# Projecting Q for pairs of batches with 288 moving columns, with output pieces at alternating rates and half-unit score banks

## The chip, the cores and the metric

The kernel runs on one core of one Trainium2 chip. The metric is device time in microseconds (us) of that core. Executions fall into a fast and a slower state.

Names used below. TensorE is the matmul engine (PE in the profile, PEld for its weight loads), DVE the vector engine, ACT the scalar engine, POOL the GpSimd engine, SyncE (SP, SPq) the engine that issues all DMAs. A *unit* is one head of one batch of one problem: 2 problems x 16 batches x 16 heads = 512 units. A *K window* is the DMA that transposes K of 16 units, a *V slot* holds V of two units. An *output piece* is one 448-column matmul of the last projection. A matmul streams *moving columns* past weights loaded before. *pp* and *ps* are the two steps in which POOL adds up the probabilities of a unit before the sum matmul reads them. The *slack* of a load is the time from its landing to its first use. "The switch" is the stretch, units 224 to 287, in which the second problem's weights replace the first's.

## The reference

```python
# twice, for A and for B, with their own inputs; B=16, Sq=144, D=448, H=16, Sk=512, Dh=256, bf16
q = (x @ wq).reshape(B, Sq, H, Dh).transpose(0, 2, 1, 3)
scores = einsum("bhqd,bhkd->bhqk", q, k_cache) * (Dh ** -0.5)
p = softmax(scores, axis=-1)
o = einsum("bhqk,bhkd->bhqd", p, v_cache)
out = o.transpose(0, 2, 1, 3).reshape(B, Sq, H * Dh) @ wo
# result: concatenate([out_A, out_B], axis=-1)
```

## The kernel before

The program is recorded once into a list per engine by a small scheduler, which also derives every semaphore wait; each engine then plays its list in order. Per unit TensorE does eight matmuls of 144 columns for Q, eight for the scores, eight for P times V, one that sums the probabilities, and on average 2.25 output pieces. The parts that the change touches (cuts marked with `# ...`):

```python
LQ, LS = 6, 2                       # Q runs 6 units ahead of PV, the scores 2
NV, NXG = 9, 2                      # 9 V slots; 2 x slots of XB batches
XB = 4 if Bn % 4 == 0 else (2 if Bn % 2 == 0 else 1)
NQT, NPT, NPP, NPS, NRI, NOST, NRUN = 6, 3, 2, 3, 2, 2, 32
# ... PSUM: qp_ps 1 bank, s_ps 2 x 2 banks, ot_ps 2, op_ps 1: all 8 banks

def t_q(U):                          # Q of one unit: 8 matmuls of 144 columns
    for kc in range(4):
        for dc in range(2):
            t.matmul(qp_ps[:, dc * SQ:(dc + 1) * SQ], lhsT=wq_sb[:, kc, c0:c0 + 128],
                     rhs=xt_sb[:, xsl, kc, xo:xo + SQ], start=(kc == 0 and dc == 0), stop=(kc == 3), ...)
def t_evac_q(U):                     # DVE: 288 elements per partition, PSUM to SBUF
    v.tensor_copy(qt_sb[:, U % NQT, :, :], src)

def t_exp(U):                        # ACT: one exp of 576 elements over two score banks
    a.activation(pt_sb[:, psl, ...], s_ps[bank][:, :, 0:2 * SQ], AF.Exp, scale=DH ** -0.5)

def t_presum(U):                     # POOL: adds the four key chunks of P, in two steps
    g.tensor_tensor(pp_sb[:, pl, :, :], pt_sb[:, psl, 0:2, :], pt_sb[:, psl, 2:4, :], op=ALU.add)
    g.tensor_tensor(ps_sb[:, sl, :], pp_sb[:, pl, 0, :], pp_sb[:, pl, 1, :], op=ALU.add)

# the loop that fixes the order, i = unit of PV
while True:
    # ... DMA issues that are due at i, stores
    t_q(i + LQ); t_evac_q(i + LQ)
    t_s(i + LS); t_exp(i + LS); t_presum(i + LS)
    t_pv(i); t_sum(i)                # the sum matmul reads ps_sb
    t_recip(i); t_check(i); t_evac_ot(i)   # ACT Ln, Exp; DVE check, ring multiply
    credit += OP_RATE                # 1.15 x the mean number of output pieces per unit
    # ... emit output pieces, two at a time, while credit and ready pieces last;
    # ... each fourth piece of the first problem's last chunk issues one of the second's eight wo loads
```

At the end every engine reads a flag and branches over a fallback path; SyncE waits for the last stores before it branches.

## Time and profile before

| | before |
|---|---|
| time, median of 3 runs | 1091.85 us (1091.58 to 1093.75) |
| span of the profiled execution | 1095.4 us |
| TensorE busy | 95% |

The head of the page of the kernel before: the span, the busy time of each engine with its share and number of instructions, and the chain of waits by engine.

```profile
span 1095.4 us, 33206 instructions
...
PE 1036.4 (95%) x13952; PEld 924.4 (84%) x13952; DVE 657.9 (60%) x2215; ACT 620.3 (57%) x1573; POOL 623.3 (57%) x1029
...
PE 88%; SPq 7%; DMA 3%; DVE 1%; ACT 1%; issue 0%; DVEq 0%
```

TensorE is the limit: it is on 88% of the chain that ended last, and every other engine is under 61% busy. But busy time does not say how tightly matmuls follow one another. The timeline of TensorE does (start and duration in us, then engine, line, operation, tiles and count):

```profile
499.82 0.35 PE L1111 MATMUL op_ps<-wo_sb,ring 128*128 128x448 bf16 x1
500.01 0.66 PE L940 MATMUL qp_ps<-xt_sb,wq_sb 128*128 128x144 bf16 x8
500.51 0.66 PE L965 MATMUL s_ps<-qt_sb,kt_sb 128*128 128x144 bf16 x8
501.01 0.66 PE L1012 MATMUL ot_ps<-pt_sb,v_sb 128*128 128x144 bf16 x8
```

Read the starts, not the durations (which overlap). Eight 144-column matmuls take 0.50 us from start to start, 62.5 ns each; the output piece took 499.82 to 500.01, 0.19 us. Both are columns / 2.4 GHz + 2.5 ns. This gives a ruler: take each matmul's start, subtract it from the next one's start, and subtract columns / 2.4 GHz + 2.5 ns. What is left is time that TensorE lost there, to a wait or to a lowered clock. I call it *lost time* below. In the kernel before, from 120 to 540 us, the lost time is 0.1 us in all. It lies elsewhere:

| us | sum of columns/2.4 + 2.5 ns | before first matmul | start (units 0 to 63) | switch (units 224 to 287) | all other units | from the last matmul's start to the end | span |
|---|---|---|---|---|---|---|---|
| before | 1017.7 | 11.0 | 41.0 | 16.8 | 0.5 | 8.3 | 1095.4 |

What the losses at the switch are made of is in the list of waits (engine, tile and line, who ended the wait: total us, times, longest):

```profile
PE s_ps L965 <- DMA kt_sb<-in_B_k_cache_dram: 6.7, 1, 6.7
...
PE qp_ps L940 <- DMA wq_sb<-in_B_wq_dram: 2.3, 1, 2.3
PE ot_ps L1012 <- DMA v_sb<-in_B_v_cache_dram: 2.1, 2, 1.9
```

Most of the rest of the 16.8 us, 3.9 us, is half clock: after these idle stretches 64 matmuls run at half the pace, those of 144 columns starting 120 ns apart instead of 62.5. Finally the groups of instructions that the change edits (line, engine, operation, tiles, shape, count; busy us, mean ns of one; idle before them and what ended it):

```profile
L987 POOL TENSOR_TENSOR pp_sb<-pt_sb 128x288 f32<-128x288 bf16 x512 | 373.1, 729 | 419.1 <-ACT pt_sb L977 418.9
L977 ACT ACTIVATE pt_sb<-s_ps 128x576 bf16<-128x576 f32 x512 | 332.9, 650 | 433.0 <-PE s_ps L965 433.0
...
L991 POOL TENSOR_TENSOR ps_sb<-pp_sb 128x144 bf16<-128x144 f32 x512 | 249.9, 488 | 40.1
L952 DVE CAST qt_sb<-qp_ps 128x288 bf16<-128x288 f32 x512 | 225.0, 440 | 44.1 <-PE qp_ps L940 41.3
```

Off TensorE everything has room: POOL needs 729 + 488 ns in a unit of about 2 us, the cast 440 ns.

### The profile page before, as it was taken

Reading aid. Unit: us, or ns where it says so; the run is one execution under the profiler, and the core shown is the slowest. Engines: PE = TensorE matmul, PEld = TensorE weight load, DVE = VectorE, ACT = ScalarE, POOL = GpSimd, SP = SyncE. Lnnn points to the kernel's source line nnn. Section 1 sums busy time; section 2 is a strip of 40 time slices with the busy share of each in tenths; the row PEclk is TensorE's granted clock in tenths of the full one; section 3 lists DMA queues with packets and bytes.
Section 4 is the critical chain, followed back from the end, with each engine's and each line's share of the span. In section 5 each row is a group of like instructions: output and inputs, shape, how many; then the busy total and the mean of one; then the engine's idle time right before and its main releaser. Section 6 shows DMA issues by size and latency. Waiting matters only on the chain.

```text
span 1095.4 us, 33206 instructions
## 1 busy us (share of the span) xinstructions
PE 1036.4 (95%) x13952; PEld 924.4 (84%) x13952; DVE 657.9 (60%) x2215; ACT 620.3 (57%) x1573; POOL 623.3 (57%) x1029
## 2 busy tenths in 40 slices
PE   1859999999999999999999799999999999999997
PEld 1858888888988889999988688889998888999995
DVE  1526666666666666666656446666666666666663
ACT  0526565565655665666656445566665556666663
POOL 0526555556655566666646446566665655666663
PEclk9969999999999999999999989999999999999999
DMA  9999999999999999999999999999999999999930
GB/s 231 297 322 275 256 279 283 281 275 284 267 265 289 280 282 276 293 282 266 259 301 311 279 288 290 286 285 286 294 287 254 278 260 269 270 288 264 261 137 13
DMA packets 631519, 294.20 MB, mean 269 GB/s; under 512 B 549440, under 2 KB 562240, under 8 KB 631360
## 3 DMA queue, kind: packets, MB, share of 16 engines
q1 hardware_dynamic: 631360, 291.99, 110.1%
q8 instruction: 111, 1.82, 0.7%
q14 instruction: 48, 0.39, 0.1%
HBM read 148.90 MB, written 4.13 MB: 140 GB/s over the span
## 4 chain that ended last, share of the span: by engine, by line
PE 88%; SPq 7%; DMA 3%; DVE 1%; ACT 1%; issue 0%; DVEq 0%
PE ot_ps L1012 22%; PE qp_ps L940 22%; PE s_ps L965 22%; PE op_ps L1111 19%; SPq L915 5%; PE ot_ps L1024 3%; DMA v_sb<-in_A_v_cache_dram 1%; DMA wq_sb<-in_B_wq_dram 1%; DMA v_sb<-in_B_v_cache_dram 1%; SPq L925 1%; SPq L894 1%; PE qp_ps L1111 1%; DVE run_sb L1069 0%; ACT pt_sb L977 0%; DVE qt_sb L952 0%
## 5 line engine op out<-in xcount | busy, mean ns | idle before, releaser
L987 POOL TENSOR_TENSOR pp_sb<-pt_sb 128x288 f32<-128x288 bf16 x512 | 373.1, 729 | 419.1 <-ACT pt_sb L977 418.9
L977 ACT ACTIVATE pt_sb<-s_ps 128x576 bf16<-128x576 f32 x512 | 332.9, 650 | 433.0 <-PE s_ps L965 433.0
L1069 DVE TENSOR_REDUCE run_sb<-ot_ps 1x1 bf16<-1x144 f32 x1024 | 262.2, 293 | 384.2 <-ACT ln_sb L1035 384.2
L940 PEld LDWEIGHTS qp_ps<-xt_sb,wq_sb 128*128 128x128 bf16 x4096 | 293.0, 99 | 113.9 <-issue 27.5
L940 PE MATMUL qp_ps<-xt_sb,wq_sb 128*128 128x144 bf16 x4096 | 345.7, 228 | 29.3 <-DMA wq_sb<-in_A_wq_dram 24.0
L965 PE MATMUL s_ps<-qt_sb,kt_sb 128*128 128x144 bf16 x4096 | 343.9, 228 | 12.6 <-DMA kt_sb<-in_B_k_cache_dram 6.7
L1012 PE MATMUL ot_ps<-pt_sb,v_sb 128*128 128x144 bf16 x4096 | 343.1, 227 | 9.2 <-DMA v_sb<-in_A_v_cache_dram 7.1
L965 PEld LDWEIGHTS s_ps<-qt_sb,kt_sb 128*128 128x128 bf16 x4096 | 277.9, 99 | 13.7 <-DMA kt_sb<-in_B_k_cache_dram 6.9
L1012 PEld LDWEIGHTS ot_ps<-pt_sb,v_sb 128*128 128x128 bf16 x4096 | 276.8, 99 | 10.7 <-DMA v_sb<-in_A_v_cache_dram 7.7
L1111 PE MATMUL op_ps<-wo_sb,ring 128*128 128x448 bf16 x1120 | 285.1, 353 | 0.0
L991 POOL TENSOR_TENSOR ps_sb<-pp_sb 128x144 bf16<-128x144 f32 x512 | 249.9, 488 | 40.1
L952 DVE CAST qt_sb<-qp_ps 128x288 bf16<-128x288 f32 x512 | 225.0, 440 | 44.1 <-PE qp_ps L940 41.3
L1055 DVE TENSOR_TENSOR ring<-ot_ps,rinv_sb 128x288 bf16<-128x288 f32 (+2 forms) x640 | 231.0, 375 | 0.0
L1040 ACT ACTIVATE rinv_sb<-ln_sb 128x144 f32<-128x144 f32 x512 | 165.4, 323 | 16.2
L1035 ACT ACTIVATE ln_sb<-ot_ps 128x144 f32<-128x144 f32 x512 | 148.6, 290 | 14.8 <-PE ot_ps L1024 14.8
L1024 PE MATMUL ot_ps<-ps_sb,ones 128*128 128x144 bf16 x512 | 116.3, 227 | 0.0
L1111 PEld LDWEIGHTS op_ps<-wo_sb,ring 128*128 128x128 bf16 x1120 | 94.0, 98 | 21.4 <-DVE ring L1055 0.4
L1024 PEld LDWEIGHTS ot_ps<-ps_sb,ones 128*128 128x128 bf16 x512 | 50.4, 98 | 0.0
L1129 ACT ACTIVATE ost_sb<-op_ps 128x448 bf16<-128x448 f32 x35 | 18.5, 529 | 2.4 <-PE op_ps L1111 2.3
L1111 PE MATMUL qp_ps<-wo_sb,ring 128*128 128x448 bf16 x32 | 7.2, 352 | 0.0
L1111 PEld LDWEIGHTS qp_ps<-wo_sb,ring 128*128 128x128 bf16 x32 | 3.1, 98 | 2.9
L1075 DVE TENSOR_REDUCE runs_sb<-run_sb 1x1 f32<-1x32 bf16 x32 | 4.5, 169 | 0.0
(13 smaller groups left out, 5.1 us busy)
## 6 DMA issues: line engine op xcount, KB each, us to landing
v_sb<-in_A_v_cache_dram SPq DMA_DIRECT2D x128, 512.0 KB, 8.0
v_sb<-in_B_v_cache_dram SPq DMA_DIRECT2D x128, 512.0 KB, 6.8
out_dram<-ost_sb SPq DMA_DIRECT2D x36, 112.0 KB, 6.3
wo_sb<-in_A_wo_dram SPq DMA_DIRECT2D x8, 448.0 KB, 7.1
wo_sb<-in_B_wo_dram SPq DMA_DIRECT2D x8, 448.0 KB, 8.4
wq_sb<-in_A_wq_dram SPq DMA_DIRECT2D x4, 768.0 KB, 6.8
wq_sb<-in_B_wq_dram SPq DMA_DIRECT2D x4, 768.0 KB, 9.0
wq_sb<-in_A_wq_dram SPq DMA_DIRECT2D x4, 128.0 KB, 7.6
```

The costliest lines, as they stand in the source:

```text
L940: ins = t.matmul(qp_ps[:, dc * SQ:(dc + 1) * SQ], lhsT=wq_sb[:, kc, c0:c0 + 128], rhs=xt_sb[:, xsl, kc, xo:xo + SQ], start=(kc == 0 and dc ...
L952: return v.tensor_copy(qt_sb[:, sl, :, :], src)
L965: ins = t.matmul(s_ps[bank][:, c // 2, (c % 2) * SQ:(c % 2 + 1) * SQ], lhsT=kt_sb[:, 2 * c + dc, ko:ko + 128], rhs=qt_sb[:, U % NQT, dc, : ...
L977: return a.activation(pt_sb[:, psl, :, :].rearrange("p (a b) q -> p a (b q)", a=2), s_ps[bank][:, :, 0:2 * SQ], AF.Exp, scale=DH ** -0.5)
L987: return g.tensor_tensor(pp_sb[:, pl, :, :], pt_sb[:, psl, 0:2, :], pt_sb[:, psl, 2:4, :], op=ALU.add)
L991: return g.tensor_tensor(ps_sb[:, sl, :], pp_sb[:, pl, 0, :], pp_sb[:, pl, 1, :], op=ALU.add)
L1012: ins = t.matmul(ot_ps[ob][:, dc * SQ:(dc + 1) * SQ], lhsT=v_sb[:, vsl, j, c * DH + dc * 128:c * DH + (dc + 1) * 128], rhs=pt_sb[:, sl, c, ...
L1024: return t.matmul(ot_ps[ob][:, 2 * SQ:3 * SQ], lhsT=ones[:, :], rhs=ps_sb[:, sl, :], start=True, stop=True)
L1040: return a.activation(rinv_sb[:, sl, :], ln, AF.Exp, scale=-1.0)
L1055: ins = v.tensor_tensor(ring[:, 2 * h:2 * h + 2, r0:r0 + q1 - q0], ot_ps[ob][:, 0:2 * SQ].rearrange("p (c q) -> p c q", c=2)[:, :, q0:q1], ...
L1069: return v.tensor_reduce(run_sb[0:1, k, j:j + 1], ot_ps[ob][0:1, 2 * SQ:3 * SQ], axis=AX.X, op=op)
L1111: ins = t.matmul(acc[0:m, 0:D], lhsT=ring[:, c, col0:col0 + m], rhs=wo_sb[:, c, :], start=(c == first), stop=(c == last))
```

## The change

The intent: the same wq block serves two batches, so project Q for an even batch and the odd one after it together, with 288 moving columns per weight load: half the Q matmuls and half their weight loads. Even batches then carry all of Q, odd ones none, and the output pieces are given rates of 0.3 (even) and 2.0 (odd) to level the load. Q for 16 waiting heads needs 19 q slots and a second Q bank in PSUM. To pay for them, the score banks shrink to three of half a unit (with two exps of 288 elements per unit), x keeps one slot for two, pp one for two, ps two for three, and Ln shares its buffer with the reciprocal. With two ps buffers, the presum of a unit must be recorded after the sum matmul two units back, whose buffer it takes, so it moves behind the sum in the loop. Apart from that, SyncE's wait for the last stores moves behind the branch.

```diff
-    LQ, LS = 6, 2
+    LQ, LS = 4, 2
-    NV, NXG = 9, 2
+    NV, NXG = 9, 1
-    NQT, NPT, NPP, NPS, NRI, NOST, NRUN = 6, 3, 2, 3, 2, 2, 32
+    NQ0, NPT, NPS, NRI, NOST, NRUN = 3, 3, 2, 2, 2, 32
 ...
-        qt_sb = sb("qt_sb", [128, NQT, 2, SQ], BF16)
+        qt_sb = sb("qt_sb", [128, NQ0 + H, 2, SQ], BF16)
-        pp_sb = sb("pp_sb", [128, NPP, 2, SQ], F32)
+        pp_sb = sb("pp_sb", [128, 2, SQ], F32)
-        qp_ps = ps("qp_ps", [128, 512], F32)
-        s_ps = [ps("s_ps%d" % i, [128, 2, 512], F32) for i in range(2)]
+        qp_ps = ps("qp_ps", [128, 2, 512], F32)
+        s_ps = [ps("s_ps%d" % i, [128, 512], F32) for i in range(3)]
 ...
-                for kc in range(4):
-                    for dc in range(2):
+                for dc in range(2):
+                    for kc in range(4):
                         c0 = h * DH + dc * 128
-                        ins = t.matmul(qp_ps[:, dc * SQ:(dc + 1) * SQ], lhsT=wq_sb[:, kc, c0:c0 + 128],
-                                       rhs=xt_sb[:, xsl, kc, xo:xo + SQ], start=(kc == 0 and dc == 0),
-                                       stop=(kc == 3), skip_group_check=True)
+                        ins = t.matmul(qp_ps[:, dc, 0:2 * SQ], lhsT=wq_sb[:, kc, c0:c0 + 128],
+                                       rhs=xt_sb[:, xsl, kc, xo:xo + 2 * SQ], start=(kc == 0), stop=(kc == 3))
 ...
-                return v.tensor_copy(qt_sb[:, sl, :, :], src)
+                return v.tensor_copy(qt_sb[:, a:b + 1:b - a, :, :],
+                                     qp_ps[:, :, 0:2 * SQ].rearrange("p e (u q) -> p u e q", u=2))
 ... (scores and exps per half unit, bank = (2 * U + k) % 3; one pp buffer; Ln into rinv_sb)
 ... (the wq loads, one batch earlier)
-                lo = pr * NU - H + 4 * hg + 4 - LQ if pr > 0 else s_min
+                lo = pr * NU - 2 * H + 4 * hg + 4 - LQ if pr > 0 else s_min
 ...
-        OP_RATE = 1.15 * NCH * NWO / NU
+        OP_RATE = tuple(f * NCH * NWO / NU for f in (0.3, 2.0, 1.2))
 ...
-            if 0 <= u < NT:
+            if 0 <= u < NT and u // H % 2 == 0:
                 t_q(u)
 ...
                 t_s(u)
-                t_exp(u)
-                t_presum(u)
 ...
                 t_sum(u)
+                if u + LS < NT:
+                    t_presum(u + LS)
 ...
-                credit += OP_RATE
+                credit += OP_RATE[i // H % 2 if i >= 4 * H else 2]
 ...
-                if eng_name == SP:
-                    drain_stores(eng, outs)
                 with eng.If(bad > 0):
+                    if eng_name == SP:
+                        drain_stores(eng, outs)
 ...
+                if eng_name == SP:
+                    drain_stores(eng, outs)
```

More of the change, by code (lines that the diff above doesn't have):

```diff
@@ L779, in bass_concat_heads__mha_block_cached__gqa_block_cached__near_ridge_kernel @@
     assert (SQ, D, SK, DH) == (144, 448, 512, 256), (SQ, D, SK, DH)
-    assert H % 4 == 0
+    assert H % 4 == 0 and Bn % 2 == 0
     NU = Bn * H
@@ L791, in bass_concat_heads__mha_block_cached__gqa_block_cached__near_ridge_kernel @@
     NWG = NWO // WOG
-    LQ, LS = 6, 2
+    LQ, LS = 4, 2
     KW, KR = 16, 32
-    NV, NXG = 9, 2
+    NV, NXG = 9, 1
     assert KR % KW == 0 and NU % KW == 0
-    XB = 4 if Bn % 4 == 0 else (2 if Bn % 2 == 0 else 1)
-    NQT, NPT, NPP, NPS, NRI, NOST, NRUN = 6, 3, 2, 3, 2, 2, 32
+    XB = 4 if Bn % 4 == 0 else 2
+    NQ0, NPT, NPS, NRI, NOST, NRUN = 3, 3, 2, 2, 2, 32
     RS = 3
@@ L822, in bass_concat_heads__mha_block_cached__gqa_block_cached__near_ridge_kernel @@
         xt_sb = sb("xt_sb", [128, NXG, 4, XB * SQ], BF16)
-        qt_sb = sb("qt_sb", [128, NQT, 2, SQ], BF16)
+        qt_sb = sb("qt_sb", [128, NQ0 + H, 2, SQ], BF16)
         pt_sb = sb("pt_sb", [128, NPT, 4, SQ], BF16)
         ones = sb("ones", [128, 128], BF16)
-        pp_sb = sb("pp_sb", [128, NPP, 2, SQ], F32)
+        pp_sb = sb("pp_sb", [128, 2, SQ], F32)
         ps_sb = sb("ps_sb", [128, NPS, SQ], BF16)
-        ln_sb = sb("ln_sb", [128, NRI, SQ], F32)
         rinv_sb = sb("rinv_sb", [128, NRI, SQ], F32)
@@ L926, in t_load_v, with q_slot @@
             S.add(SP, e, writes=[(("v", sl), G)], dma_sem="v%d" % sl, name="v%d" % G)
+        def q_slot(U):
+            pr, b, h = unit(U)
+            return NQ0 + h if b % 2 else ((pr * Bn + b) // 2 * H + h) % NQ0
         def t_q(U):
@@ L947, in t_evac_q @@
         def t_evac_q(U):
-            sl = U % NQT
-            src = qp_ps[:, 0:2 * SQ].rearrange("p (c q) -> p c q", c=2)
+            a, b = q_slot(U), q_slot(U + H)
             def e(v):
-                return v.tensor_copy(qt_sb[:, sl, :, :], src)
-            S.add(DVE, e, reads=[("qp", ("q", U))], writes=[(("qt", sl), U)], banks=["qp"], name="eq%d" % U)
+                return v.tensor_copy(qt_sb[:, a:b + 1:b - a, :, :],
+                                     qp_ps[:, :, 0:2 * SQ].rearrange("p e (u q) -> p u e q", u=2))
+            S.add(DVE, e, reads=[("qp", ("q", U))], writes=[(("qt", a), U), (("qt", b), U + H)], banks=["qp"],
+                  name="eq%d" % U)
         def t_s(U):
@@ L958, in t_s, with e, x @@
             ko = U % KR * 128
-            bank = U % 2
-            def e(t):
-                ins = None
-                for c in range(4):
-                    for dc in range(2):
-                        ins = t.matmul(s_ps[bank][:, c // 2, (c % 2) * SQ:(c % 2 + 1) * SQ],
-                                       lhsT=kt_sb[:, 2 * c + dc, ko:ko + 128],
-                                       rhs=qt_sb[:, U % NQT, dc, :], start=(dc == 0), stop=(dc == 1))
-                return ins
-            S.add(PE, e, reads=[(("qt", U % NQT), U), (("kt", ksl), W)], writes=[(("sp", bank), U)],
-                  banks=["s%d" % bank], name="S%d" % U)
-        def t_exp(U):
-            bank = U % 2
-            psl = U % NPT
-            def e(a):
-                return a.activation(pt_sb[:, psl, :, :].rearrange("p (a b) q -> p a (b q)", a=2),
-                                    s_ps[bank][:, :, 0:2 * SQ], AF.Exp, scale=DH ** -0.5)
-            S.add(ACT, e, reads=[(("sp", bank), U)], writes=[(("pt", psl), U)], banks=["s%d" % bank], name="ex%d" % U)
+            qsl = q_slot(U)
+            psl = U % NPT
+            for k in range(2):
+                bank = (2 * U + k) % 3
+                def e(t, k=k, bank=bank):
+                    ins = None
+                    for c in (2 * k, 2 * k + 1):
+                        for dc in range(2):
+                            ins = t.matmul(s_ps[bank][:, (c % 2) * SQ:(c % 2 + 1) * SQ],
+                                           lhsT=kt_sb[:, 2 * c + dc, ko:ko + 128],
+                                           rhs=qt_sb[:, qsl, dc, :], start=(dc == 0), stop=(dc == 1))
+                    return ins
+                S.add(PE, e, reads=[(("qt", qsl), U), (("kt", ksl), W)], writes=[(("sp", bank), 2 * U + k)],
+                      banks=["s%d" % bank], name="S%d.%d" % (U, k))
+            for k in range(2):
+                bank = (2 * U + k) % 3
+                def x(a, k=k, bank=bank):
+                    return a.activation(pt_sb[:, psl, 2 * k:2 * k + 2, :].rearrange("p b q -> p (b q)"),
+                                        s_ps[bank][:, 0:2 * SQ], AF.Exp, scale=DH ** -0.5)
+                S.add(ACT, x, reads=[(("sp", bank), 2 * U + k)], writes=[(("pt", psl), U)], banks=["s%d" % bank],
+                      name="ex%d.%d" % (U, k))
         def t_presum(U):
@@ L983, in t_presum @@
             sl = U % NPS
-            pl = U % NPP
             def e1(g):
-                return g.tensor_tensor(pp_sb[:, pl, :, :], pt_sb[:, psl, 0:2, :], pt_sb[:, psl, 2:4, :], op=ALU.add)
-            S.add(POOL, e1, reads=[(("pt", psl), U)], writes=[(("pp", pl), U)], name="pp%d" % U)
+                return g.tensor_tensor(pp_sb[:, :, :], pt_sb[:, psl, 0:2, :], pt_sb[:, psl, 2:4, :], op=ALU.add)
+            S.add(POOL, e1, reads=[(("pt", psl), U)], writes=[("pp", U)], name="pp%d" % U)
             def e2(g):
-                return g.tensor_tensor(ps_sb[:, sl, :], pp_sb[:, pl, 0, :], pp_sb[:, pl, 1, :], op=ALU.add)
-            S.add(POOL, e2, reads=[(("pp", pl), U)], writes=[(("ps", sl), U)], name="ps%d" % U)
+                return g.tensor_tensor(ps_sb[:, sl, :], pp_sb[:, 0, :], pp_sb[:, 1, :], op=ALU.add)
+            S.add(POOL, e2, reads=[("pp", U)], writes=[(("ps", sl), U)], name="ps%d" % U)
         def ring_cols(pr, b):
@@ L1031, in t_recip @@
             sl = U % NRI
-            ln = ln_sb[:, sl, :]
+            ln = rinv_sb[:, sl, :]
             def e1(a):
                 return a.activation(ln, ot_ps[ob][:, 2 * SQ:3 * SQ], AF.Ln)
-            S.add(ACT, e1, reads=[(("sum", ob), U)], writes=[(("ln", sl), U)], banks=["ot%d" % ob],
+            S.add(ACT, e1, reads=[(("sum", ob), U)], writes=[(("rinv", sl), (U, 0))], banks=["ot%d" % ob],
                   name="ln%d" % U)
@@ L1040, in e2 @@
                 return a.activation(rinv_sb[:, sl, :], ln, AF.Exp, scale=-1.0)
-            S.add(ACT, e2, reads=[(("ln", sl), U)], writes=[(("rinv", sl), U)], name="rc%d" % U)
+            S.add(ACT, e2, reads=[(("rinv", sl), (U, 0))], writes=[(("rinv", sl), U)], name="rc%d" % U)
         def t_evac_ot(U):
@@ L1103, in t_op_piece @@
             col0 = (r % RS) * 128
-            acc = op_ps if bank == "op" else qp_ps
+            acc = op_ps if bank == "op" else qp_ps[:, 0, :]
             key = "opp" if bank == "op" else "qp"
@@ L1124, in t_evac_op @@
             sl = r % NOST
-            acc = op_ps if bank == "op" else qp_ps
+            acc = op_ps if bank == "op" else qp_ps[:, 0, :]
             key = "opp" if bank == "op" else "qp"
@@ L1152, in bass_concat_heads__mha_block_cached__gqa_block_cached__near_ridge_kernel @@
         for XG in range(NXGT):
-            lo = (XG - NXG + 1) * XB * H - LQ if XG >= NXG else s_min
+            lo = (XG - NXG + 1) * XB * H - H - LQ if XG >= NXG else s_min
             plan(lo, XG * XB * H - LQ - (1 if XG else 0), 0, t_load_x, XG)
@@ L1187, in bass_concat_heads__mha_block_cached__gqa_block_cached__near_ridge_kernel @@
         tail_bank = {NP * NCH - 1: "qp"}
+        qp_free = NT - H - LQ
         op_first, op_last = {}, {}
@@ L1225, in bass_concat_heads__mha_block_cached__gqa_block_cached__near_ridge_kernel @@
                 t_s(u)
-                t_exp(u)
-                t_presum(u)
+            if -LS <= i < 0:
+                t_presum(i + LS)
             u = i
@@ L1243, in bass_concat_heads__mha_block_cached__gqa_block_cached__near_ridge_kernel @@
                         if bank == "qp":
-                            ready = max(i + OP_DELAY, NT - LQ)
+                            ready = max(i + OP_DELAY, qp_free)
                         if u >= NT - 2:
```

## The prediction

> **What bounds the kernel now.** TensorE. The page shows PE busy 95% and 88% of the chain of waits. The timeline is stricter: groups of eight 144-column matmuls start 0.50 us apart, 62.5 ns each, 60 ns of columns at 2.4 GHz plus 2.5 ns; between 120 and 540 us the sum of gaps beyond columns/2.4 + 2.5 ns is 0.1 us. So no weight-load cost is hidden. Lost time sits elsewhere: about 41 us before 120 us (weights, K, V arriving; half clock), 17 us at 540-640 us (second problem's weights: waits on wq, K, V; half clock), 7 us after the last matmul.
>
> **What the change does.**
> - Q: 4096 matmuls of 144 columns become 2048 of 288. 2048 x 2.5 ns = -5.1 us. The Trainium skill ("TensorE: Matmul & The Clock Gate", "Wait — 56ns, not 53.3ns?") gives about 2.5 ns fixed per warm matmul; this trace agrees. All on the path.
> - The stores are awaited after the branch. SyncE's branch takes 3.6 us after the last store landed; now it overlaps: about -2 us.
> - The DVE cast grows from 288 to 576 elements: 440 ns plus 300 ns (288 elements at the slope of the ring multiply, 235 ns at 96, 335 at 192), estimate 0.74 us. A Q unit without output pieces takes PE 0.98+0.5+0.5+0.06 = 2.04 us; the loop sum -> Ln -> check -> ring multiply -> cast -> next Q then costs about 0.1 us for two such units in a row: 2 per 32 units, +0.2 to 0.35 us.
> - By the instruction order Q runs 4 units ahead, but the rate switches on the unit itself: the last 4 units of each even batch have neither Q nor (mostly) pieces: 1.06 us of PE against an ACT estimate of about 1.25 (two exps of about 0.32 start to start, Ln 0.33, Exp 0.25) and POOL about 1.30 (729+488 ns plus gaps). +0.3 to 0.5 us per 32 units.
> - These two: about +10 us in all (15 periods).
> - Switch of problems: wq loads earlier (good), but x and wq precede K window 16, whose slack was 9 us: a stall of some us near unit 254. Six of eight wo loads now queue behind K window 18, whose issue holds SyncE's queue 17-25 us, and are needed about 15 us after it starts: estimate 9-14 us stall at unit 278, plus half clock. About 20 us lost, against 17 before.
> - Start: still bound by DMA; K windows 3 to 7 have 1 to 4 us slack, which alternating batches eat: +2 to 4 us.
>
> **Sum**: -5 -2 +10 +3 +3, pulled down as the rates look tuned: 1096 us, 8 in 10 within 1083 to 1110. Faster by over 2%: 0.04; within 2%: 0.88; slower: 0.08.
>
> **What would show it.** Q matmuls 122.5 ns apart; PE matmul count 11904; cast near 0.74 us; small waits of PE on the cast in even batches; on ACT or POOL in their last quarter; an output piece waiting for DMA wo_sb of the second problem; a tail 2 us shorter.
>
> **What would make it wrong.** If wo lands before unit 278, or K issue is short (16 us), the switch gets cheaper than before and the kernel wins: about 1085. If the 4-dimensional cast is much slower than 0.74 us, or ACT takes over 1.4 us per unit, every batch pays: 1110 or more. Worse early DMA pacing would show as K and V waits after 120 us.

## The result, and the profile after

| | before | after |
|---|---|---|
| time, median of 4 runs | 1092.8 us (1091.58 to 1096.46) | 1106.41 us (1104.6 to 1107.92) |
| ratio | | 1.0118, 95% interval 1.0088 to 1.0148 |
| span of the profiled execution | 1095.4 us | 1104.5 us |

Ratios here are the mean time of one kernel's fast runs over that of the other's of the same rounds, so not quite the ratio of the medians quoted beside them. The change made the kernel about 1.2% slower, within the 2% band; the prediction had said 0.4%.

The head of the page after:

```profile
span 1104.5 us, 30556 instructions
...
PE 1037.7 (94%) x11904; PEld 864.1 (78%) x11904; DVE 646.5 (59%) x1959; ACT 677.7 (61%) x2085; POOL 625.4 (57%) x1029
...
PE 83%; SPq 7%; POOL 3%; ACT 3%; DMA 2%; issue 1%; POOLq 0%; DVE 0%; DVEq 0%
```

2048 matmuls and 2048 weight loads are gone, PEld is 60 us less busy, and the time is longer. POOL and ACT, absent or at 1% before, hold 3% each of the chain. The waits of TensorE after, without those of the first weights:

```profile
PE op_ps L1115 <- DMA wo_sb<-in_B_wo_dram: 13.8, 1, 13.8
...
PE ot_ps L1028 <- POOL ps_sb L995: 7.2, 31, 0.3
PE qp_ps L943 <- DVE qt_sb L953: 1.7, 2, 0.9
PE s_ps L971 <- DMA kt_sb<-in_B_k_cache_dram: 0.9, 1, 0.9
```

Two new kinds of wait are there: one long wait of an output piece for the second problem's wo, and 31 short ones of the sum matmul for POOL. (The list shows part of a short wait only, since a matmul's modelled end covers the rest; the lost time, taken from the starts, has all of it.) The edited groups:

```profile
L991 POOL TENSOR_TENSOR pp_sb<-pt_sb 128x288 f32<-128x288 bf16 x512 | 374.1, 731 | 381.8 <-ACT pt_sb L981 357.7
L981 ACT ACTIVATE pt_sb<-s_ps 128x288 bf16<-128x288 f32 x1024 | 363.5, 406 | 337.6 <-PE s_ps L971 337.3
...
L995 POOL TENSOR_TENSOR ps_sb<-pp_sb 128x144 bf16<-128x144 f32 x512 | 250.9, 490 | 87.9 <-PE ot_ps L1028 12.3
...
L953 DVE CAST qt_sb<-qp_ps 128x576 bf16<-128x576 f32 x256 | 191.8, 749 | 63.1 <-PE qp_ps L943 60.1
```

No instruction became slow by itself. The timeline of TensorE at the end of an even batch shows the new pattern:

```profile
462.79 1.14 PE L943 MATMUL qp_ps<-xt_sb,wq_sb 128*128 128x288 bf16 x8
463.77 0.66 PE L971 MATMUL s_ps<-qt_sb,kt_sb 128*128 128x144 bf16 x8
...
468.33 0.23 PE L1028 MATMUL ot_ps<-ps_sb,ones 128*128 128x144 bf16 x1
468.40 0.66 PE L971 MATMUL s_ps<-qt_sb,kt_sb 128*128 128x144 bf16 x8
468.90 0.66 PE L1016 MATMUL ot_ps<-pt_sb,v_sb 128*128 128x144 bf16 x8
469.73 0.24 PE L1028 MATMUL ot_ps<-ps_sb,ones 128*128 128x144 bf16 x1 [0.17 <-POOL ps_sb L995]
```

Eight Q matmuls take 0.98 us from start to start, 122.5 ns each: 288 / 2.4 + 2.5, as the ruler says. Further down, units without Q and without output pieces (*light units* below) follow each other: TensorE has 1.06 us of work in them, but the sum matmul at 469.73 starts 0.83 us after the P-times-V group that takes 0.50. The same stretch on POOL:

```profile
468.31 0.73 POOL L991 TENSOR_TENSOR pp_sb<-pt_sb 128x288 f32<-128x288 bf16 x1
469.19 0.49 POOL L995 TENSOR_TENSOR ps_sb<-pp_sb 128x144 bf16<-128x144 f32 x1
469.82 0.73 POOL L991 TENSOR_TENSOR pp_sb<-pt_sb 128x288 f32<-128x288 bf16 x1
470.69 0.49 POOL L995 TENSOR_TENSOR ps_sb<-pp_sb 128x144 bf16<-128x144 f32 x1
471.32 0.73 POOL L991 TENSOR_TENSOR pp_sb<-pt_sb 128x288 f32<-128x288 bf16 x1
```

POOL is the pace: a pp every 1.50 us, made of 0.73 + 0.49 us of work and two gaps of 0.14 to 0.15 us. Last, SyncE's queue at the switch. Before, the last of the eight wo loads stands just ahead of K window 18:

```profile
604.51 0.54 SPq L894 DMA_DIRECT2D wo_sb<-in_B_wo_dram  x1
605.10 22.93 SPq L915 DMA_TRANSPOSE kt_sb<-in_B_k_cache_dram  x1
```

After, six of them stand behind it:

```profile
596.97 23.15 SPq L914 DMA_TRANSPOSE kt_sb<-in_B_k_cache_dram  x1
...
621.31 1.62 SPq L893 DMA_DIRECT2D wo_sb<-in_B_wo_dram  x3
```

K window 18 holds the queue for 23.15 us, and the wo loads that TensorE needs at 613 us come out behind it; the third one lands at 626.94 us and the output piece starts at 626.99.

The lost time of both kernels, by the ruler (all other units split into waits of the sum matmul on POOL, waits of Q on the cast, and the rest):

| us | columns/2.4 + 2.5 ns | before first matmul | start | sum on POOL | Q on cast | other units, rest | switch | last matmul to end | span |
|---|---|---|---|---|---|---|---|---|---|
| before | 1017.7 | 11.0 | 41.0 | 0.0 | 0.1 | 0.4 | 16.8 | 8.3 | 1095.4 |
| after | 1012.6 | 10.9 | 41.9 | 8.5 | 2.7 | 0.7 | 21.7 | 5.5 | 1104.5 |
| after again, another chip | 1012.6 | 10.4 | 41.9 | 8.3 | 2.7 | 0.7 | 21.7 | 5.7 | 1104.0 |

So -5.1 for the matmuls, -2.8 at the end, +8.5 and +2.6 in ordinary units, +4.9 at the switch and +1.1 for the rest make +9.2, against 9.1 us between the spans. The timed runs differ by more, 1.18%, and part of the reason is known: the profiled execution of the kernel before took 1097.14 us, longer than any of its four timed runs, and its switch lost more than in two experiments below that leave the switch as it was (12.3 and 13.3 us), while the changed kernel's was 21.7 us both times.

### The profile page after: what moved, and what is told of

Its sections match the earlier page's. It is cut to its first block, busy times and chain, and to the rows that moved or that the text cites. A ratio compares the mean times of both kernels' runs of the same rounds, so it can differ in the third digit from the quotient of the medians.

```text
span 1104.5 us, 30556 instructions
## 1 busy us (share of the span) xinstructions
PE 1037.7 (94%) x11904; PEld 864.1 (78%) x11904; DVE 646.5 (59%) x1959; ACT 677.7 (61%) x2085; POOL 625.4 (57%) x1029
## 4 chain that ended last, share of the span: by engine, by line
PE 83%; SPq 7%; POOL 3%; ACT 3%; DMA 2%; issue 1%; POOLq 0%; DVE 0%; DVEq 0%
PE qp_ps L943 22%; PE ot_ps L1016 20%; PE s_ps L971 19%; PE op_ps L1115 19%; SPq L914 5%; PE ot_ps L1028 3%; POOL pp_sb L991 2%; POOL ps_sb L995 2%; ACT pt_sb L981 2%; DMA v_sb<-in_A_v_cache_dram 1%; ACT rinv_sb L1044 1%; SPq L924 1%; ACT rinv_sb L1039 1%; SPq L893 1%; PE qp_ps L1115 1%
## 5 line engine op out<-in xcount | busy, mean ns | idle before, releaser
L981 ACT ACTIVATE pt_sb<-s_ps 128x288 bf16<-128x288 f32 x1024 | 363.5, 406 | 337.6 <-PE s_ps L971 337.3
L971 PEld LDWEIGHTS s_ps<-qt_sb,kt_sb 128*128 128x128 bf16 x4096 | 292.0, 99 | 63.8 <-issue 9.1
L943 PE MATMUL qp_ps<-xt_sb,wq_sb 128*128 128x288 bf16 x2048 | 298.0, 289 | 13.0 <-DMA wq_sb<-in_A_wq_dram 11.3
L995 POOL TENSOR_TENSOR ps_sb<-pp_sb 128x144 bf16<-128x144 f32 x512 | 250.9, 490 | 87.9 <-PE ot_ps L1028 12.3
L1115 PE MATMUL op_ps<-wo_sb,ring 128*128 128x448 bf16 x1120 | 268.5, 354 | 13.8 <-DMA wo_sb<-in_B_wo_dram 13.8
L943 PEld LDWEIGHTS qp_ps<-xt_sb,wq_sb 128*128 128x128 bf16 x2048 | 196.3, 99 | 87.6 <-issue 11.7
L953 DVE CAST qt_sb<-qp_ps 128x576 bf16<-128x576 f32 x256 | 191.8, 749 | 63.1 <-PE qp_ps L943 60.1
L1039 ACT ACTIVATE rinv_sb<-ot_ps 128x144 f32<-128x144 f32 x512 | 149.5, 292 | 63.6 <-PE ot_ps L1028 23.4
L1044 ACT ACTIVATE rinv_sb<-rinv_sb 128x144 f32<-128x144 f32 x512 | 165.4, 323 | 16.1
L1115 PEld LDWEIGHTS op_ps<-wo_sb,ring 128*128 128x128 bf16 x1120 | 98.0, 98 | 55.6 <-DMA wo_sb<-in_B_wo_dram 14.2
```

The source lines that it names most:

```text
L943: ins = t.matmul(qp_ps[:, dc, 0:2 * SQ], lhsT=wq_sb[:, kc, c0:c0 + 128], rhs=xt_sb[:, xsl, kc, xo:xo + 2 * SQ], start=(kc == 0), stop=(kc ...
L953: return v.tensor_copy(qt_sb[:, a:b + 1:b - a, :, :], qp_ps[:, :, 0:2 * SQ].rearrange("p e (u q) -> p u e q", u=2))
L971: ins = t.matmul(s_ps[bank][:, (c % 2) * SQ:(c % 2 + 1) * SQ], lhsT=kt_sb[:, 2 * c + dc, ko:ko + 128], rhs=qt_sb[:, qsl, dc, :], start=(dc ...
L981: return a.activation(pt_sb[:, psl, 2 * k:2 * k + 2, :].rearrange("p b q -> p (b q)"), s_ps[bank][:, 0:2 * SQ], AF.Exp, scale=DH ** -0.5)
L995: return g.tensor_tensor(ps_sb[:, sl, :], pp_sb[:, 0, :], pp_sb[:, 1, :], op=ALU.add)
L1044: return a.activation(rinv_sb[:, sl, :], ln, AF.Exp, scale=-1.0)
```

## The experiments

My theory after the result: pairing pays what it promised, and the schedule built around it takes it back in three places, (a) light units in which POOL sets the pace, (b) short waits of Q on the longer cast, (c) wo loads queued behind a K window. Rivals: the 288-column Q or the 576-element cast cost by themselves; half-unit score banks cost; at the switch the DMA engines as a whole are the limit, so a wait taken away there comes back elsewhere. Four kernels stood together on one chip (e1 to e4), four on a second, two on a third, and two last. The chips differ: the kernel before had medians of 1097.54, 1094.19 and 1094.41 us on the three, so ratios are compared before times. The changed kernel did not run on the first of these chips; e1 to e3 are set against it by the lost time in their traces, one trace each. All twelve gave correct results.

### The changed kernel again (e0_after)

No edit.

> The changed kernel again, unedited, so that the others of this call stand beside it on one chip. Expected ratio to before 1.008 to 1.013; after the start 13 us of waits on POOL and the cast, 14 us on wo_sb.

Measured: 1105.84 us, ratio 1.0101 (1.0082 to 1.012); lost times in the table above. The result repeats.

### Rates in phase with Q (e1_phase)

```diff
-                credit += OP_RATE[i // H % 2 if i >= 4 * H else 2]
+                credit += OP_RATE[(i + LQ) // H % 2 if i >= 4 * H else 2]
```

> One edit in the changed kernel: the rate of output pieces switches with the Q phase (4 units earlier), so no unit lacks both Q and pieces for long. My theory: the waits of the sum matmul on POOL in units 15, 16 and 18 of each 32 (about 0.8 us per 32 units, about 9 us in all after the start) go to nearly nothing; more Q units without pieces raise the waits of Q on the DVE cast from about 3 to 5-6 us; the 14 us wait for wo_sb stays. About 7 us less than the changed kernel: 1099, ratio to before about 1.006. Rival (the 288-column Q and the 576-element cast cost by themselves, not the schedule): unchanged, ratio 1.012.

Measured: 1098.32 us, ratio 1.0009 (0.9983 to 1.0036). Lost time of the sum on POOL outside start and switch 0.0 us (from 8.5), of Q on the cast 4.1 (from 2.7), the wait for wo_sb still 15.2 us. The span is 8.3 us shorter than the changed kernel's. Four units of phase were the whole of (a), and the rival that blames the pairing itself falls. Two of the expectation's figures missed: the waits on the cast rose less than the 5 to 6 us expected, and the ratio came out lower than 1.006.

### A flat rate (e2_flat)

```diff
-        OP_RATE = tuple(f * NCH * NWO / NU for f in (0.3, 2.0, 1.2))
+        OP_RATE = tuple(f * NCH * NWO / NU for f in (1.15, 1.15, 1.15))
```

> One edit in the changed kernel: all three rates 1.15, the constant of the kernel before. My theory: POOL and cast waits after the start fall from 13 us to under 2, the wait for wo_sb disappears because the wo loads are issued before K window 18, and in its place K or V waits of up to 10 us near units 254 to 290 appear as in the kernel before: about 1085 to 1090, ratio 0.993 to 0.998. Rival A (pairing itself costs): ratio 1.008 or more. Rival B (alternating rates were needed so that K and V keep up; a flat rate makes odd batches about 24 us against 25 us of K and V issue per batch): K and V waits in odd batches through the first half, ratio above 1.005.

Measured: 1091.27 us, ratio 0.9942 (0.9915 to 0.9969). Outside start and switch the lost time is 0.0 us on POOL, 0.1 on the cast, 0.3 for the rest. No wait for wo_sb is left, but others stand in its place:

```profile
PE s_ps L971 <- DMA kt_sb<-in_B_k_cache_dram: 8.4, 2, 7.3
...
PE ot_ps L1016 <- DMA v_sb<-in_B_v_cache_dram: 2.1, 1, 2.1
```

The switch still loses 20.4 us (21.7 in the changed kernel). Both rivals fall: paired Q with a flat rate beats the kernel before, and K and V keep up with odd batches everywhere but at the switch. The ratio holds the moved wait for the stores too, which by itself is 0.9979 (e5_tail). A flat rate does not remove every light unit: between the last output piece of the first problem and the first of the second, at unit 276, there are none, and units 273 to 276 lose 0.43 to 0.44 us each to POOL at the switch. The value of pairing alone can be read here without any stall: 160 undisturbed units (319 to 479, sum matmul to sum matmul) take 317.72 us in the kernel before and 316.16 in this one, 1.56 us less; 160 units x 4 matmuls saved per unit x 2.5 ns is 1.60. The alternating rates, which were to level the load on TensorE, gain nothing in ordinary units: TensorE takes the same sum of columns in any order, as long as nothing else falls short within a unit.

### K window 18 behind the wo loads (e3_k18late)

```diff
             lo = KW * (W + 1) - KR - LS if KW * (W + 1) > KR else s_min
+            if W == NKW // 2 + 2:
+                lo += 8
```

> One edit in the changed kernel: K window 18 is issued 8 units later, so that all eight wo loads of the second problem stand before it in SyncE's queue. My theory: the 14 us wait for wo_sb falls to under 1 us; K window 18 had 23 us of slack and now lands about 15 us later against a need that comes 14 us sooner, so 0 to 6 us of K wait return. 8 to 14 us less than the changed kernel: 1093 to 1098, ratio 1.000 to 1.005. Rival (DMA is the limit at the switch, so the wait only moves to K and V): under 3 us gained, K and V waits of over 10 us near unit 286.

Measured: 1095.93 us, ratio 0.9988 (0.9959 to 1.0017). The list of waits has no wo_sb any more, and K of the second problem instead:

```profile
PE ot_ps L1028 <- POOL ps_sb L995: 7.2, 31, 0.3
PE s_ps L971 <- DMA kt_sb<-in_B_k_cache_dram: 6.8, 2, 4.6
```

The switch loses 13.5 us instead of 21.7, a third of the wait having come back as a 4.6 us wait for K window 18; POOL's waits are untouched, as they should be. So (c) was the queue order, for about 8 us. The time came out as expected, the ratio just under the 1.000 to 1.005. The start of this execution lost 44.1 us rather than 41.9, which is why the span falls by 5.4 us only.

### Half-unit score banks on the kernel before (e4_halfbanks)

```diff
-        s_ps = [ps("s_ps%d" % i, [128, 2, 512], F32) for i in range(2)]
+        s_ps = [ps("s_ps%d" % i, [128, 512], F32) for i in range(3)]
 ... (scores and exps per half unit, as in the change; everything else as before)
```

> The kernel before with one part of the change alone: three score banks of half a unit, each with its own exp of 288 columns. My theory: nothing on TensorE's path; ACT busy up by about 30 us, time within 1 us of before, ratio 0.999 to 1.002. Rival (two exps per unit delay probabilities or the reuse of a score bank): waits of S or PV matmuls after 120 us, ratio 1.004 or more.

Measured: 1096.46 us, ratio 0.9996 (0.9969 to 1.0023); lost time outside start and switch 0.3 us. The banks cost nothing. ACT is 76 us busier (696.4 against 620.3), not 30. The exps alone grew by the 32 us that I had expected (365.1 against 332.9); the other 44 are overlap that is gone: in the kernel before, the busy times of ACT's groups add up to 47 us more than ACT's busy time, here to 3 us more. It is off the path either way.

### The end alone, on the kernel before (e5_tail)

The part of the change that moves the wait for the stores behind the branch, nothing else.

> The kernel before with one part of the change alone: SyncE waits for the last stores after the branch instead of before it. My theory: the 3.6 us branch now runs while the last store is in flight; the time from the landing of the last store to the end falls from about 4 us to 2 us or less: ratio 0.997 to 0.999. Rival: the end is set by another engine or by the store itself, no change in the tail.

Measured: 1091.56 us, ratio 0.9979 (0.9958 to 0.9999). From the landing of the last store to the end 0.50 us, against 4.02; from the last matmul's start to the end 5.6 us, against 8.3. In the kernel before SyncE's branch record starts at 1091.46 us and its next one at 1095.13. That piece of the change is good for 2 to 3 us by itself.

### The presum buffers of before, in the changed kernel (e6_bufs2)

```diff
-    NV, NXG = 9, 1
+    NV, NXG = 8, 1
-    NQ0, NPT, NPS, NRI, NOST, NRUN = 3, 3, 2, 2, 2, 32
+    NQ0, NPT, NPP, NPS, NRI, NOST, NRUN = 3, 3, 2, 3, 2, 2, 32
 ... (pp_sb with NPP buffers, presum queued right after the scores, as before)
```

A first build with nine V slots ran out of on-chip memory (the two buffers take 1440 bytes per partition), so one V slot was given up.

> The changed kernel with the presum buffers of before restored (two pp, three ps, presum queued right after the scores), paid for with one V slot less (8 for 9), which may add V waits of its own, so it is read by its wait sums and not by its time. In the trace of the changed kernel POOL's period in light units is 1.50 us: 0.73 + 0.49 and two gaps of 0.14 to 0.15. Theory A (the shrunken buffers make POOL wait for itself): the period falls to about 1.30 and the waits of the sum matmul on POOL from 0.8 us to under 0.3 us per 32 units. Theory B (POOL's own work is the limit): period above 1.4, waits over 0.6 us per 32 units.

Measured: 1105.06 us, ratio 1.0094. More is lost at the start (47.5 us), and at the switch TensorE waits 9.9 us for V at unit 252; all three kernels with eight V slots lose 47 us or more at the start, those with nine at most 44.2. Lost time of the sum on POOL: 0.0 us. POOL in the same light units:

```profile
469.24 0.73 POOL L992 TENSOR_TENSOR pp_sb<-pt_sb 128x288 f32<-128x288 bf16 x1
470.05 0.49 POOL L996 TENSOR_TENSOR ps_sb<-pp_sb 128x144 bf16<-128x144 f32 x1
470.50 0.73 POOL L992 TENSOR_TENSOR pp_sb<-pt_sb 128x288 f32<-128x288 bf16 x1
471.31 0.49 POOL L996 TENSOR_TENSOR ps_sb<-pp_sb 128x144 bf16<-128x144 f32 x1
471.75 0.73 POOL L992 TENSOR_TENSOR pp_sb<-pt_sb 128x288 f32<-128x288 bf16 x1
```

A pp every 1.25 us: the next pp starts 0.45 us after a ps of 0.49, so the two overlap, where in the changed kernel it started 0.63 us after. Theory A holds: in light units POOL was held up by its own shrunken buffers and not by its work.

### Which buffer (e9_pp2, e10_ps3)

e9_pp2 has two pp buffers and the rest as changed, e10_ps3 three ps buffers, with the presum back in its earlier place, and one pp. Both have eight V slots.

> One look, read by POOL's period and waits, not by its time (8 V slots): the changed kernel with two pp buffers, the two ps buffers and the late presum left as changed. If the single pp buffer is what makes POOL wait for itself, its period in light units is about 1.25 to 1.30 us as with all buffers restored, and the sum matmul's waits on POOL outside start and switch fall from 8.5 us to under 2. If the two ps buffers are to blame (a ps must wait for the sum matmul two units back), they stay over 6 us.

> The counterpart: three ps buffers and the presum queued right after the scores, the single pp buffer left as changed (8 V slots). If the single pp buffer is to blame: period about 1.4 to 1.5 us and waits on POOL of 5 us or more outside start and switch. If the ps buffers are: about 1.25 us and under 2.

| | POOL period in light units | gap pp to ps | gap ps to next pp | lost, sum on POOL |
|---|---|---|---|---|
| changed (one pp, two ps) | 1.50 us | 0.14 us | 0.14 us | 8.5 us |
| e10_ps3 (one pp, three ps) | 1.44 us | 0.08 us | 0.14 us | 2.4 us |
| e9_pp2 (two pp, two ps) | 1.32 us | 0.14 us | -0.04 us | 0.0 us |
| e6_bufs2 (two pp, three ps) | 1.25 us | 0.08 us | -0.04 us | 0.0 us |

The single pp buffer costs 0.18 to 0.19 us per unit (1.50 - 1.32, 1.44 - 1.25), because the next pp may not start before the ps that reads the buffer has completed. The two ps buffers cost 0.06 to 0.07 us, because each ps then has a second semaphore to wait for, that of the sum matmul two units back. TensorE itself is not late there: in the changed kernel the ps that starts at 469.19 us waits for a sum matmul that started at 466.89. So the first is the larger. The period of e10_ps3 (1.44 us) is the one expected if the pp buffer is to blame, and e9_pp2's loss went as expected for it, its period ending just above the 1.25 to 1.30 us. But e10_ps3 missed its 5 us or more of loss: a gain of 0.06 us in the period took away 6 us of loss. The loss is not proportional to the period: TensorE enters a stretch of light units with POOL ahead, and only what is left when that lead is used up becomes a wait. In the changed kernel's stretch shown above, ps is ready 2.95 us before its sum matmul starts at the twelfth unit of the even batch and 0.17 us before it at the fifteenth.

### Rates that alternate only before the switch (e7_hybrid, e7b_hybrid)

```diff
-        OP_RATE = tuple(f * NCH * NWO / NU for f in (0.3, 2.0, 1.2))
+        OP_RATE = tuple(f * NCH * NWO / NU for f in (0.3, 2.0, 1.15))
-                credit += OP_RATE[i // H % 2 if i >= 4 * H else 2]
+                credit += OP_RATE[(i + LQ) // H % 2 if NU - 2 * H - LQ <= i < NU - LQ else 2]
```

> The changed kernel with a flat rate of 1.15, except that the 32 units before the second problem keep the alternating rates in phase with Q, so that the odd batch in which K window 16 must arrive lasts about 30 us instead of 24, and the wo loads still stand before K window 18. My theory: no waits on POOL or the cast outside those 32 units, wait for K window 16 down from 7.5 us to 1 to 4 us, no wait for wo_sb: 4 to 8 us under the flat rate, ratio to before 0.986 to 0.991. Rival (the switch is limited by DMA in all): the wait moves to K 17 or 18 or V and the ratio stays at 0.993 or more.

> The hybrid kernel again, beside the version with two x slots on the same chip: ratio to before 0.992 to 0.996, about 14 us lost in the 64 units around the switch, of which about 5 us on K window 16.

Measured: 1087.66 us, ratio 0.9942 (0.992 to 0.9963), and the second time 1087.45 us, ratio 0.9933 (0.9905 to 0.9961). The switch loses 15.4 and 13.7 us, K window 16 being waited for 4.4 and 4.5 us instead of 7.5. By the traces, that is 5.0 to 6.7 us less lost at the switch than with the flat rate, as expected. By the clock the gain over the flat rate is not shown: its ratio, taken on another chip, was 0.9942 as well, the ratio expected here was 0.986 to 0.991, and the rival's mark (0.993 or more) was met. The two did not run on one chip, and the flat rate's trace is of the slowest of its six runs.

### Two x slots of two batches (e8_xpairs)

```diff
-    NV, NXG = 9, 1
+    NV, NXG = 9, 2
-    XB = 4 if Bn % 4 == 0 else 2
+    XB = 2
-            lo = (XG - NXG + 1) * XB * H - H - LQ if XG >= NXG else s_min
+            lo = (XG - NXG + 1) * XB * H - LQ if XG >= NXG else s_min
 ... (x of the second pair is loaded at the start; rates as in the hybrid)
```

> The hybrid rates plus x in two slots of two batches (the same memory as one slot of four): the changed kernel has one x slot, so the second problem's first x load can only start once the last pair of batches is projected and its issue holds SyncE's queue 12 us right before K window 16. Here x of the first pair goes before K window 15 and x of the second before K window 17. My theory (this single slot is what makes K window 16 late): K window 16 issues about 12 us earlier, its wait (about 5 us with the V wait behind it in the hybrid) goes to under 1 us, 3 to 6 us less than the hybrid kernel: ratio to before 0.988 to 0.991. Rival (DMA as a whole is the limit at the switch): the wait reappears at K 17, K 18 or V, ratio within 0.002 of the hybrid kernel's.

Measured: 1088.62 us, ratio 0.9937 (0.991 to 0.9965), the hybrid's 0.9933. This theory of mine fell. SyncE's queue, first in the hybrid kernel (second run), then here:

```profile
525.30 10.78 SPq L904 DMA_TRANSPOSE xt_sb<-in_B_x_dram  x1
536.12 1.95 SPq L905 DMA_TRANSPOSE xt_sb<-in_B_x_dram  x1
538.11 16.50 SPq L914 DMA_TRANSPOSE kt_sb<-in_B_k_cache_dram  x1
```

```profile
529.52 25.47 SPq L914 DMA_TRANSPOSE kt_sb<-in_B_k_cache_dram  x1
```

K window 16 is issued 8.6 us earlier and occupies the queue 9.0 us longer: 538.11 + 16.50 = 554.61 in the one, 529.52 + 25.47 = 554.99 in the other. It lands at 556.7 and 557.0 us. The four wq loads still stand before it. TensorE then waits 2.8 us for K window 16 instead of 4.5, but 3.1 us for K window 18 instead of 1.3: the wait has come back there, as the rival said, and the loss at the switch is 15.4 us, not less. So the rival holds here: an earlier issue buys nothing while K arrives no sooner. The DMA engines are as busy before the switch as in it (a mean share of 1.08 to 1.21 in the stretches of the hybrid's second trace that I looked at between 300 and 800 us), so the busy share does not tell what is special at the switch, and where the limit sits inside the DMA path stays open.

What the switch costs with its loads in a good order: 12.3 to 16.8 us in the versions with Q of before, 13.5 in e3_k18late, 13.7 to 15.4 in the hybrid and this one. It is not all DMA supply: in the hybrid and this one 2.0 us of it are waits of the sum matmul on POOL.

## Why the prediction was right or wrong

The time lay in the range and the class was right; the centre was 10 us too low. Point by point:

- *"2048 x 2.5 ns = -5.1 us ... All on the path."* Right: Q matmuls start 122.5 ns apart, there are 11904 matmuls, and 160 undisturbed units are 1.56 us shorter in e2_flat. The Trainium skill ("TensorE: Matmul & The Clock Gate", section "Wait — 56ns, not 53.3ns?") states this cost of about 2.5 ns per warm matmul, and the trace agrees at 144, 288 and 448 columns. From this follows why the gain is so small: fewer matmuls save only the fixed part. Halving the weight loads saved nothing beside it, since they did not set the spacing of the matmuls before.
- *"The stores are awaited after the branch ... about -2 us."* Right, a little low: 2.8 us from the last matmul's start to the end, and the ratio 0.9979 alone.
- *"estimate 0.74 us"* for the cast and *"+0.2 to 0.35 us"* per 32 units for the waits behind it. Right: 749 ns, and 2.7 us in the 12 such periods outside start and switch, 0.22 us each.
- *"the last 4 units of each even batch have neither Q nor (mostly) pieces ... an ACT estimate of about 1.25 ... and POOL about 1.30 (729+488 ns plus gaps). +0.3 to 0.5 us per 32 units."* The place was right and the size was not: 8.5 us over the same 12 periods is 0.7 us each. The term that was mis-sized is POOL's period, 1.50 us and not 1.30. I took the gaps from the kernel before, with its two pp and three ps buffers; e6_bufs2, e9_pp2 and e10_ps3 show that the change's own smaller buffers add 0.18 to 0.19 us (pp) and 0.06 to 0.07 us (ps), and that with the old buffers, or two pp buffers alone, the loss is nothing. ACT did not bind.
- *"Six of eight wo loads now queue behind K window 18 ... estimate 9-14 us stall at unit 278 ... About 20 us lost, against 17 before."* Right for the changed kernel: a wait of 13.8 us, 2.8 us near unit 254, and 21.7 us lost in all. The base was probably off: the 16.8 us are of one execution of the kernel before, slower than its timed runs; with the same switch, e4_halfbanks and e5_tail lost 12.3 and 13.3.
- *"Start: ... K windows 3 to 7 have 1 to 4 us slack, which alternating batches eat: +2 to 4 us."* Wrong. The start lost 0.9 us more, and from K window 3 on the slack grew: window 3 landed 12.2 us ahead of its first use instead of 1.7, windows 4 to 7 by 8.0 to 15.6 instead of 2.2 to 4.2. I had not looked at where the x loads went: with one slot, x of the next four batches moved behind K window 3, which was issued at 105.7 us instead of 116.3 and landed 4.5 us earlier; the other 6 us of its slack come from a first use at 143.8 us instead of 137.8. How far the order is the cause stays open: no run tested it alone, and in e8_xpairs, with x of two batches again just ahead of K window 3, the window was issued at 112.8 us and still had 11.1 us of slack.
- *"pulled down as the rates look tuned."* This step failed outright. The terms add up to +9, about 1101 us from 1091.85; the 5 us I took off came from a guess about the author and no trace. e2_flat (0.9942, against 1.0101 to 1.0118) shows that the alternation was worse than the constant rate it replaced.

Of the 10 us between 1096 and 1106.4, about 5 are that guess. The rest, an estimate from the lost times: the POOL term (10.0 us in the 14 periods after the start, 1.5 of them at the switch, where the middle of its range made 6: about +4) and what else the switch lost against a typical base (about +4), less the start, which did not come (about -2), and about a microsecond at the end. That the total lay in the range is in part luck: an unsupported -5 and terms that erred both ways.

## What to carry to other kernels

When TensorE already runs at columns / clock + a few ns, fewer and wider matmuls save only those few ns each; work out that number first and weigh it against the buffers that the wider form takes from other stages. Spreading TensorE's load differently over units gained nothing here in ordinary units, but stretches of little work do harm: each must be checked against the slowest other engine *with the buffers it will have then*, and phase (who runs how many units ahead) must be counted in. A load that is needed soon must not stand in one queue behind a transpose that holds the queue for 16 to 28 us; and a load issued earlier gains nothing if it does not land earlier, as in e8_xpairs. Here paired Q with a flat rate, alternating only ahead of the switch, came to 0.993 to 0.994 of the kernel before (about 0.2% of that from the moved wait for the stores), and to about 1.6% under the changed kernel on the chip that ran both. All these differences lie within the 2% band.

## What the Trainium skill lacked or had wrong

- "TensorE: Matmul & The Clock Gate", section "Back-to-back issue gap": it gives about 81 ns per matmul at N=128 and about 131 ns at N=512 for a sustained stream of weight load and matmul pairs, and says that the N/2.4 + 2.5 formula holds for isolated ones. Here the formula held for thousands in a row, each with a weight load of its own: 62.5 ns at 144 columns, 122.5 at 288, 0.19 us at 448.
- "Perfetto Trace Analysis", section "Identifying the Most-Contended Engine": it names LDWEIGHTS busy, beside the share of peak FLOPs, as a measure of how near TensorE is to its limit. PEld went from 84% to 78% between the two kernels here, and none of that was headroom: the matmul spacing was set by columns in both.
- "Perfetto Trace Analysis", section "What \"DMA-bound\" means": solid DMA slices on the issuing sequencer's track are said to be descriptor generation and not data movement. The issue of one and the same K transpose took 16.5 us or 25.5 us here, and ended at nearly the same moment, 554.6 and 555.0 us, after starting 8.6 us apart. So the length of such a slice is not set by the transfer alone; that it contains waiting for the DMAs before it is likely and not shown. I found on no page how long a large DMA transpose holds its queue (15.9 to 28.4 us for 16 units of K in these runs).
- "Runtime: NRT & Kernel Launch", section "Instruction fetch mechanics": it warns that a taken branch out of the prefetched pages stalls, without a figure. Here 3.7 us passed between SyncE's branch over the fallback path and its next record (1091.46 to 1095.13), and 2.7 us in e4_halfbanks (1088.46 to 1091.15); it cost nothing once it overlapped the last store. That this is the stall of the page is not shown.
- No page that I read has the cost of a semaphore wait between two dependent POOL instructions: 0.08 us from pp to ps with one wait, 0.14 us with two, and 0.14 us from ps to pp against an overlap of 0.04 us without one.
